# The query projection of a decode kernel, computed as rows in four column tiles and brought back to columns

## The chip, the cores and the metric

One core of one Trainium2 chip. The metric is device time in microseconds of one execution, as the median of several executions. The profiles are of single executions; their span is about 1.2 us shorter than the device time.

In the views, PE is the matrix engine and PEld its loading of weights; DVE, ACT and POOL are the vector, scalar and GpSimd engines; SPq is the queue of the engine that issues the loads. PSUM is the memory that PE writes its sums to, in banks. Times in a view, and all times of single packets and clock records told here, are us from the start of the span.

## The reference

One token attends over a cache of 65,536 keys, and an MLP mixer runs beside it. Only the first line below is touched by the change.

```python
q = ((x @ wq).reshape(B, Sq, Hq, Dh)).transpose(0, 2, 1, 3)   # x: 1x1x1024, wq: 1024x4096, 32 heads of 128
k = jnp.repeat(k_cache, rep, axis=1); v = jnp.repeat(v_cache, rep, axis=1)   # 4 KV heads, 65536 keys, rep = 8
scores = jnp.einsum("bhqd,bhkd->bhqk", q, k) * (Dh ** -0.5)
p = _softmax(scores, axis=-1)
o = jnp.einsum("bhqk,bhkd->bhqd", p, v)
# ... then o @ wo, and to it is added  x + B(layernorm(x)),  B a mixer MLP with w1, w2, w3, w4
```

Everything is bf16. K and V are 67 MB each, the weights together some 36 MB, and each byte is read once.

## The kernel before

The four first loads are issued at once, in one queue: both halves of wq into the second buffers of K and V, then the first K and V loads of 4 MB. A K or V load covers a pair of tiles; there are 32 tiles of 8,192 keys and 16 pairs.

```python
load_rows(Kn[:, 1, :], b_K[1], "wqa", A_wq, 0, 4)      # first half of wq, 4 MB
load_rows(Vn[:, 1, :], b_V[1], "wqb", A_wq, 4, 4)      # second half
issue_k(0)
issue_v(0)
# ... constants, layer norm of x ...
def mm_cols(ps_tile, c0, ncols, lhs_fn, rhs_fn, j0, nj, njt, bufs, b_ps):
    fns = []
    for j in range(j0, j0 + nj):
        for cx in range(ncols):
            fns.append(lambda e, j=j, cx=cx: e.matmul(ps_tile[:, c0 + cx:c0 + cx + 1], lhs_fn(j - j0, cx), rhs_fn(j),
                                                      start=(j == 0 and cx == 0), stop=(j == njt - 1), skip_group_check=True))
    _grp(q_pe, fns, reads=bufs, writes=[b_ps], partial=(j0 > 0))

for j0, t in ((0, Kn), (4, Vn)):       # 2 x 128 products: a 128x128 block of wq stationary, one column of x moving
    mm_cols(M1_ps, 0, HQ, ..., j0, 4, KT_D, (b_K[1] if j0 == 0 else b_V[1]) + [b_xn], b_M1)
issue_k(1)                             # second K load: its buffer held wq's first half
issue_v(1)
_op(q_dve, lambda e: e.tensor_copy(qT_bf[:], M1_ps[:, 0:HQ]), reads=[b_M1], writes=[b_qT])   # "q's cast"
# ... Yall from q (16 DVE products), layer norm for the MLP ...
for n in range(NT):                    # per tile: transposes of K on DVE (Ttr), scores on PE (QK), softmax, PV on PE
    QK(n); Ttr(n + 1, [0]); stats1(n); ...; PV(n); FLASH(n)
    # ... MLP and output weights are loaded and used in between ...
    if n % 2 == 0:
        issue_k(n // 2 + 2)            # a K buffer is free when the pair's transposes are done
    else:
        issue_v(n // 2 + 2)            # a V buffer when the pair's PV products are done
```

## Time and profile before

| | before |
|---|---|
| device time, median (3 runs) | 402.97 us (402.88 to 403.31) |
| DMA: bytes, share of 16 engines | 169.87 MB, 98.4% |
| busy: DVE, PE, POOL, ACT | 57%, 47%, 15%, 12% |
| q's cast | 27.91 us |
| third K load issued | 49.71 us |
| last weights used | 398.80 us |

The page of the kernel before, parts 2 and 3 (40 slices of 10 us, in tenths; then what DMA moved in each):

```profile
DMA  8999999999999999999999999999999999999995
q1 hardware_dynamic: 6920, 169.87, 98.4%
HBM read 169.87 MB, written 0.00 MB: 423 GB/s over the span
```

The table of windows (start:end, length, busy time and instructions of PE, PEld, DVE, ACT and POOL, then granted clock, DMA share, GB/s):

```profile
0.00:50.00 50.00, 14.74 (x308) 10.89 (x313) 18.95 (x54) 2.66 (x4) 6.42 (x29) 1.00 0.98 415
50.00:100.00 50.00, 20.73 (x215) 6.96 (x209) 30.34 (x53) 6.67 (x19) 8.17 (x9) 1.00 1.01 433
...
300.00:350.00 50.00, 21.42 (x194) 7.72 (x196) 33.94 (x55) 6.85 (x19) 6.88 (x8) 0.60 0.99 429
350.00:402.00 52.00, 28.98 (x320) 11.97 (x322) 23.86 (x43) 6.27 (x17) 8.67 (x9) 0.57 0.90 385
```

DMA never pauses: only the first and the last slice are below 9 tenths, and the rate is flat at some 430 GB/s. DVE, the busiest engine, has two fifths of the span to spare. (The granted clock of 1.00 in the first windows is not a measurement: the trace has no clock record before 105 us in this execution. The score products at 40.30 us below take the same 1.90 us as most do later under a recorded clock of 0.50.)

The timeline of the front (start, length, engine, line, operation, output<-inputs, count, idle time before it and what ended it):

```profile
18.73 3.55 PE L366 MATMUL M_ps<-xn_bf,Kn 128*128 128x1 bf16 x128 [0.57 <-DVE maskT L356]
22.38 0.33 SPq L286 DMA_DIRECT2D Kn<-in_A_k_cache_dram  x1
22.74 2.45 PE L366 MATMUL M_ps<-xn_bf,Vn 128*128 128x1 bf16 x86 [0.46 <-DMA Vn<-in_A_wq_dram]
26.59 1.28 PE L366 MATMUL M_ps<-xn_bf,Vn 128*128 128x1 bf16 x42 [1.39 <-issue]
27.91 0.19 DVE L375 CAST qT_bf<-M_ps 128x32 bf16<-128x32 f32 x1 [8.90 <-PE M_ps L366]
35.54 5.74 DVE L463 STREAM_TRANSPOSE X<-Kn 128x1024 f32<-128x1024 f32 x5
40.30 1.90 PE L475 MATMUL S_ps<-X,Yall 128*32 128x512 bf16 x16 [5.97 <-DVE X L463]
43.88 1.28 ACT L505 ACT_TABLE_LOAD   x1 [43.88 <-DVE brun L501]
49.71 0.33 SPq L286 DMA_DIRECT2D Kn<-in_A_k_cache_dram  x1
52.86 1.25 DVE L463 STREAM_TRANSPOSE X<-Kn 128x1024 f32<-128x1024 f32 x1 [3.23 <-DMA Kn<-in_A_k_cache_dram]
```

The projection waits for wq's second half, has a hole of 1.4 us, and its result goes through Yall and a layer norm to the first tile. But DVE, having done its first two tiles, then waits 3.23 us for the second K load.

The chain of waits (start, length, what), and the largest of DVE's waits (engine and tile, waited for: total us, times, longest):

```profile
22.74 2.45 PE M_ps L366 x86
25.20 1.39 issue
...
49.71 27.42 DMA Kn<-in_A_k_cache_dram
77.15 1.25 DVE X L463
```

```profile
DVE X L463 <- DMA Kn<-in_A_k_cache_dram: 64.5, 11, 10.0
```

The chain does pass through the projection. It says so because it follows each wait to its releaser: the transposes at 77.15 waited for a load that was issued at 49.71, and the issue waited for the first tiles. It does not say that the 27.42 us between are mostly time in a queue (its 4 MB need some 10 us at the rate of the windows).

### The profile page before, as it was taken

Reading aid. Unit: us, or ns where it says so; the run is one execution under the profiler, and the core shown is the slowest. Engines: PE = TensorE matmul, PEld = TensorE weight load, DVE = VectorE, ACT = ScalarE, POOL = GpSimd, SP = SyncE. Lnnn points to the kernel's source line nnn. Section 1 sums busy time; section 2 is a strip of 40 time slices with the busy share of each in tenths; the row PEclk is TensorE's granted clock in tenths of the full one; section 3 lists DMA queues with packets and bytes.
Section 4 is the critical chain, followed back from the end, with each engine's and each line's share of the span. In section 5 each row is a group of like instructions: output and inputs, shape, how many; then the busy total and the mean of one; then the engine's idle time right before and its main releaser. Section 6 shows DMA issues by size and latency. Waiting matters only on the chain.

```text
span 401.6 us, 5142 instructions
## 1 busy us (share of the span) xinstructions
PE 187.7 (47%) x2043; PEld 84.2 (21%) x2059; DVE 227.8 (57%) x400; ACT 48.4 (12%) x127; POOL 62.0 (15%) x90
## 2 busy tenths in 40 slices
PE   0361445064525745275630966353433545344674
PEld 0250111021103511062110731121111311111142
DVE  0217666277806588255753387676836775778410
ACT  0000211011101011011110011111201111112100
POOL 5000013011211011110310102111110102122110
PEclk9999999999855565555565555665565855656556
DMA  8999999999999999999999999999999999999995
GB/s 353 431 416 433 447 421 419 447 436 421 441 441 420 419 441 437 424 434 436 428 426 444 436 421 428 442 434 427 424 450 418 439 441 424 421 428 431 437 420 217
DMA packets 7088, 170.20 MB, mean 424 GB/s; under 512 B 916, under 2 KB 920, under 8 KB 1048
## 3 DMA queue, kind: packets, MB, share of 16 engines
q1 hardware_dynamic: 6920, 169.87, 98.4%
q8 instruction: 16, 0.26, 0.2%
q14 instruction: 8, 0.07, 0.0%
q10 hardware_dynamic: 144, 0.00, 0.0%
HBM read 169.87 MB, written 0.00 MB: 423 GB/s over the span
## 4 chain that ended last, share of the span: by engine, by line
DMA 54%; DVE 24%; PE 17%; issue 2%; ACT 2%; another core or an unknown queue 1%; SPq 0%; POOL 0%; ACTq 0%
DMA Kn<-in_A_k_cache_dram 43%; DVE X L463 12%; DMA Kn<-in_B_w_dram 6%; DMA Vn<-in_A_wq_dram 5%; PE H_ps L366 4%; DVE pT_f L516 3%; PE S_ps L475 3%; PE OT_ps L523 3%; DVE mrow L482 3%; PE M_ps L366 2%; ACT p_sb L505 2%; PE PT_ps L514 1%; PE M_ps L551 1%; PE OUT_ps L391 1%; DVE Yall L380 1%
## 5 line engine op out<-in xcount | busy, mean ns | idle before, releaser
L463 DVE STREAM_TRANSPOSE X<-Kn 128x1024 f32<-128x1024 f32 x128 | 151.7, 1215 | 64.5 <-DMA Kn<-in_A_k_cache_dram 64.5
L523 PE MATMUL OT_ps<-Vn,pT_f 128*32 128x512 bf16 x512 | 59.9, 620 | 54.1 <-DVE pT_f L516 54.1
L475 PE MATMUL S_ps<-X,Yall 128*32 128x512 bf16 x512 | 58.0, 598 | 17.0 <-DVE X L463 17.0
L488 PE MATMUL MB_ps<-Rm,Lmat 128*128 128x16 bf16 x32 | 6.2, 193 | 87.7 <-DVE Rm L483 87.7
L537 POOL TENSOR_TENSOR O_acc<-O_acc,tmpO 128x513 f32<-128x513 f32 x28 | 32.9, 1176 | 89.1 <-ACT tmpO L531 89.1
L535 POOL TENSOR_SCALAR O_acc<-O_acc,ff 128x513 f32<-128x513 f32 x28 | 19.6, 700 | 150.7 <-ACT ff L510 150.7
L505 ACT ACTIVATE p_sb<-S_ps,brun 128x512 bf16<-128x512 f32 x32 | 22.0, 688 | 173.1 <-DVE brun L503 154.6
L482 DVE TENSOR_REDUCE mrow<-S_ps 128x1 f32<-128x512 f32 x32 | 21.6, 674 | 24.6 <-PE S_ps L475 24.6
L531 ACT ACTIVATE tmpO<-OT_ps 128x512 f32<-128x512 f32 x32 | 19.2, 598 | 107.8 <-PE OT_ps L523 107.8
L475 PEld LDWEIGHTS S_ps<-X,Yall 128*32 128x32 bf16 x512 | 16.5, 126 | 54.7 <-DVE X L463 38.6
L516 DVE STREAM_TRANSPOSE pT_f<-PT_ps 128x512 f32<-128x512 f32 x32 | 22.9, 716 | 7.8 <-PE PT_ps L514 4.2
L523 PEld LDWEIGHTS OT_ps<-Vn,pT_f 128*32 128x32 bf16 x512 | 14.6, 128 | 59.4 <-DVE pT_f L516 42.7
L488 PEld LDWEIGHTS MB_ps<-Rm,Lmat 128*128 128x128 bf16 x32 | 3.3, 103 | 112.2 <-DVE Rm L483 112.2
L514 PE MATMUL PT_ps<-p_sb,permR 128*128 128x512 bf16 x16 | 9.5, 594 | 21.2 <-ACT p_sb L505 21.2
L366 PEld LDWEIGHTS H_ps<-xn_bf,W 128*128 128x128 bf16 x224 | 14.4, 172 | 1.7 <-issue 1.7
L366 PE MATMUL H_ps<-xn_bf,W 128*128 128x1 bf16 x224 | 14.5, 202 | 0.0
L514 PEld LDWEIGHTS PT_ps<-p_sb,permR 128*128 128x128 bf16 x32 | 3.4, 106 | 42.4 <-ACT p_sb L505 42.4
L492 DVE TENSOR_REDUCE Bst<-MB_ps 128x1 f32<-128x16 f32 x32 | 5.6, 174 | 8.3 <-PE MB_ps L488 8.3
L330 PE MATMUL M_ps<-ln_s,ones_f 128*128 128x1 f32 x6 | 1.8, 362 | 17.5 <-DVE ln_s L329 17.5
L533 POOL COPY O_acc<-tmpO 128x513 f32<-128x513 f32 x4 | 2.5, 615 | 47.5 <-ACT tmpO L531 47.5
L551 PE MATMUL M_ps<-O_acc,cb_W 128*128 128x128 f32 x32 | 7.4, 403 | 2.0 <-DVE cb_W L544 2.0
L391 PE MATMUL OUT_ps<-Kn,gh_bf 128*1 128x256 bf16 x112 | 5.8, 370 | 3.5 <-DMA Kn<-in_B_w_dram 3.5
(101 smaller groups left out, 114.0 us busy)
## 6 DMA issues: line engine op xcount, KB each, us to landing
Kn<-in_A_k_cache_dram SPq DMA_DIRECT2D x15, 4096.0 KB, 27.4
Vn<-in_A_v_cache_dram SPq DMA_DIRECT2D x15, 4096.0 KB, 22.3
W<-in_B_w_dram SPq DMA_DIRECT2D x2, 3584.0 KB, 25.1
W<-in_A_wo_dram SPq DMA_DIRECT2D x3, 2048.0 KB, 23.2
Kn<-in_A_wq_dram SPq DMA_DIRECT2D x1, 4096.0 KB, 12.3
Vn<-in_A_wq_dram SPq DMA_DIRECT2D x1, 4096.0 KB, 21.4
W<-in_B_w_dram SPq DMA_DIRECT2D x2, 2048.0 KB, 32.2
Kn<-in_A_k_cache_dram SPq DMA_DIRECT2D x2, 2048.0 KB, 24.8
```

The lines of the kernel that those rows point to most:

```text
L366: fns.append(lambda e, j=j, cx=cx: e.matmul(ps_tile[:, c0 + cx:c0 + cx + 1], lhs_fn(j - j0, cx), rhs_fn(j), start=(j == 0 and cx == 0), st ...
L463: _op(q_dve, lambda e, ix=ix: e.transpose(out=X32[:, xs, 1024 * ix:1024 * (ix + 1)], in_=Kn32[:, s, 4096 * half + 1024 * ix:4096 * half + ...
L475: fns.append(lambda e, we=we, cm=cm, mv=mv: e.matmul(S_ps[32 * cm:32 * cm + 32, :], Yall[:, h, we, :, :].rearrange("p a g -> p (a g)"), mv ...
L482: _op(q_dve, lambda e: e.reduce_max(mrow[:, m:m + 1], S_ps[:, :], axis=AX.X), reads=[b_S], writes=[b_mrow[m]])
L505: _op(q_act, lambda e: e.activation(p_sb[:, m, :], S_ps[:, :], ACTF.Exp, bias=brun[:, kn:kn + 1], scale=SCALE, accum_out=tmpO[:, m, 512:513]),
L514: _op(q_pe, lambda e: e.matmul(PT_ps[:, :], permR[:, :], p_sb[:, m, :], start=True, stop=True), reads=[b_p[m], b_const], writes=[b_PT])
L516: _op(q_dve, lambda e: e.transpose(out=pT_f[:, :], in_=PT_ps[:, :]), reads=[b_PT], writes=[b_pT])
L523: fns.append(lambda e, q=q, q4=q4: e.matmul(OT_ps[32 * q4:32 * q4 + 32, :], pT_bf[:, q, :, 1], Vn[:, s, 8192 * half + 512 * q:8192 * half ...
L531: _op(q_act, lambda e: e.activation(tmpO[:, m, 0:512], OT_ps[:, :], ACTF.Copy), reads=[b_OT], writes=[b_tmpO[m]], partial=True)
L535: _op(q_pool, lambda e: e.tensor_scalar(out=O_acc[:, :], in0=O_acc[:, :], scalar1=ff[:, m:m + 1], scalar2=0.0, op0=ALU.mult, op1=ALU.add), ...
L537: _op(q_pool, lambda e: e.tensor_tensor(out=O_acc[:, :], in0=O_acc[:, :], in1=tmpO[:, m, :], op=ALU.add), reads=[b_tmpO[m]], writes=[b_Oacc])
L551: fns.append(lambda e, t=t: e.matmul(M0_ps[:, 128:256], cb_W[:, t, :, :].rearrange("p g i -> p (g i)"), O_acc[:, t * P:(t + 1) * P], start ...
```

## The change

The intent is to spend less of PE's front on the projection. 256 products of one moving column, each with a fresh 128x128 block of wq as weights, become 64 products in which wq moves, 512 columns at a time, and x is the stationary side, broadcast to 32 columns. Four column tiles work at once, on four bands of 512 outputs, into two PSUM banks. q then lies in rows, so DVE and ACT each copy one bank, and eight products against columns of the identity matrix select one row of each band and bring q back to columns. The loads and their order stay as they were.

```diff
-        for j0, t in ((0, Kn), (4, Vn)):
-            mm_cols(M1_ps, 0, HQ, lambda j, cx, t=t: t[:, 1, j * HQD + cx * P:j * HQD + (cx + 1) * P], lambda j: xn_bf[:, j:j + 1], j0, 4, KT_D,
-                    (b_K[1] if j0 == 0 else b_V[1]) + [b_xn], b_M1)
+        q_banks = ((PT_ps, b_PT), (OT_ps, b_OT))
+        for j0, t, bt in ((0, Kn, b_K[1]), (4, Vn, b_V[1])):
+            fns = []
+            for j in range(j0, j0 + 4):
+                for b in range(2):
+                    for jj in range(4):
+                        fns.append(lambda e, j=j, b=b, jj=jj, j0=j0, t=t: e.matmul(
+                            q_banks[b][0][32 * jj:32 * jj + 32, :], xn_bf[:, j:j + 1].broadcast_to([P, 32]),
+                            t[:, 1, (j - j0) * HQD + 512 * (4 * b + jj):(j - j0) * HQD + 512 * (4 * b + jj + 1)],
+                            start=(j == 0), stop=(j == KT_D - 1), tile_position=(0, 32 * jj)))
+            _grp(q_pe, fns, reads=bt + [b_xn], writes=[b_PT, b_OT], partial=(j0 > 0))
         issue_k(1)
         issue_v(1)
+        _op(q_dve, lambda e: e.tensor_copy(p_sb[:, 0, :], PT_ps[:, :]), reads=[b_PT], writes=[b_p[0]])
+        _op(q_act, lambda e: e.activation(p_sb[:, 1, :], OT_ps[:, :], ACTF.Copy), reads=[b_OT], writes=[b_p[1]])
+        _grp(q_pe, [lambda e, b=b, i=i: e.matmul(M1_ps[:, 16 * b + i:16 * b + 16:4], p_sb[:, b, P * i:P * i + P], ident_bf[:, 0:97:32],
+                                                 start=(b + i == 0), stop=True, skip_group_check=True)
+                    for b in range(2) for i in range(4)], reads=b_p + [b_const], writes=[b_M1])
         _op(q_dve, lambda e: e.tensor_copy(qT_bf[:], M1_ps[:, 0:HQ]), reads=[b_M1], writes=[b_qT])
```

## The prediction

> **What bounds the kernel now.** DMA, nearly from end to end. The page gives 169.87 MB read at 423 GB/s over the 401.6 us span, the main queue's packets filling 98.4% of 16 engines. The table of windows shows 429 to 433 GB/s and a DMA share of 0.99 to 1.01 in every 50 us stretch from 50 to 350 us. The Trainium skill ("DMA: Bandwidth & Descriptors", "Where 436 GB/s comes from") puts the fabric's ceiling at 435.2 GB/s; this trace agrees, at 433. The time is about 2 us before the first big packet, 395 us of transfers without a gap, and 4 us from the last weights to the output. DVE is busy 57%, PE 47%; DVE waits 64.5 us for K tiles (the waits).
>
> **The touched stage** (timeline). PE multiplies the first half of wq from 18.70 to 22.28 us (128 one-column products), waits for the second half (22.74), multiplies it in 2.45 + 1.28 us around a hole of 1.48 us (released by "issue"); DVE casts q at 27.91. Then Yall (3.57 us), a layer norm, the first K transposes (35.5), the first score products (40.3).
>
> **Costs.**
> - Removed: 256 one-column products with 128-column weight loads, 7.28 us of PE, and probably the 1.48 us hole.
> - Added: 64 products of 512 columns, four column tiles at once: 16 rounds. The score products have this form: 16 products, 4 rounds, in 1.90 us, starts 0.43 us apart, as the skill ("TensorE: Matmul & The Clock Gate", Part 2, "Back-to-back issue gap": N/1.2 ns cold) states for 512 columns. Estimate: 3.6 us for the first half; 3.6 for the second, or 1.9 if the clock rises (some score groups take 0.97 to 1.3 us in the chain).
> - Added after it: two PSUM copies in parallel on DVE and ACT, 0.6 to 0.7 us (a 512-column ACT copy takes 0.60, a 512-column DVE reduction from PSUM 0.67), and eight selecting products, about 0.4.
> - Moved: ACT's first instruction becomes a copy at about 26 us, so the 1.28 us table load before the first exponential (43.9) may go there, off that chain.
>
> Sum: q's cast at 26 to 28 us instead of 27.91, first scores at 38.5 to 40.5, release of the first K buffer (third K load, issued at 49.71) 0 to 3 us earlier.
>
> **On the critical path: nothing, I expect.** The chain passes through these products, but then through 27.42 us of DMA after the K load issued at 49.71. Its 4 MB need about 10 us at 432 GB/s; the other 17 are queueing. The shortest such landing in the chain is 19.48 us, still 9 us of queue. The loads issued at 22.38 and 27.95 stand behind 16 MB that fill the queue until about 42 us. An earlier issue only waits longer. Bytes and tail (last weights at 398.8) are untouched.
>
> **Predicted:** 402.9 us, 80% range 402.1 to 403.7. Faster by over 2%: 0.01; within 2%: 0.98; slower: 0.01.
>
> **What would show it.** Right: 429 to 433 GB/s in the same windows; DVE's wait for K tiles grows by what the front saves; the second K tile (52.9) and the last weights (398.8) land within 0.5 us of before. A step is wrong if a projection half takes over 4.5 us, the hole stays, a second table load appears, or q's cast comes after 28.5.
>
> **What would make it wrong.** A late release that empties the queue (a DMA share under 0.9 over several us past 50), a front later by over 9 us, or wider PE reads lowering the DMA rate.

## The result, and the profile after

The changed kernel takes 402.95 us (402.77 to 403.10, 6 runs); the kernel before took 402.95 us (402.86 to 403.31, 6 runs). The ratio is 0.9999, with a 95% interval from 0.9986 to 1.0012: the same. Ratios here and below are the mean time of one kernel's runs over that of the other's of the same rounds, so not quite the ratio of the medians quoted.

The page after, the same lines:

```profile
DMA  8999999999999999999999999999999999999994
q1 hardware_dynamic: 6920, 169.87, 98.4%
HBM read 169.87 MB, written 0.00 MB: 423 GB/s over the span
```

The windows after:

```profile
0.00:50.00 50.00, 14.69 (x136) 6.29 (x137) 19.65 (x55) 3.25 (x5) 7.02 (x30) 0.78 0.98 417
50.00:100.00 50.00, 18.91 (x199) 6.54 (x201) 30.43 (x53) 6.77 (x20) 7.54 (x8) 0.57 1.00 432
...
300.00:350.00 50.00, 22.93 (x198) 8.19 (x204) 34.19 (x55) 7.11 (x19) 6.87 (x8) 0.57 1.00 430
350.00:402.00 52.00, 27.01 (x320) 10.79 (x318) 23.61 (x42) 6.00 (x17) 8.63 (x9) 0.60 0.90 383
```

The timeline of the front after; L376 is the new projection, each row four products that run at once:

```profile
17.88 0.62 PE L376 MATMUL PT_ps<-Kn,xn_bf 128*32 128x512 bf16 x4
18.28 0.64 PE L376 MATMUL OT_ps<-Kn,xn_bf 128*32 128x512 bf16 x4
...
22.54 0.40 PE L376 MATMUL PT_ps<-Vn,xn_bf 128*32 128x512 bf16 x4 [1.24 <-DMA Vn<-in_A_wq_dram]
22.77 0.39 PE L376 MATMUL OT_ps<-Vn,xn_bf 128*32 128x512 bf16 x4
...
24.51 0.69 DVE L383 CAST p_sb<-PT_ps 128x512 bf16<-128x512 f32 x1 [5.70 <-PE OT_ps L376]
25.66 0.19 DVE L388 CAST qT_bf<-M_ps 128x32 bf16<-128x32 f32 x1 [0.46 <-PE M_ps L385]
33.28 5.74 DVE L476 STREAM_TRANSPOSE X<-Kn 128x1024 f32<-128x1024 f32 x5
46.17 0.33 SPq L286 DMA_DIRECT2D Kn<-in_A_k_cache_dram  x1
52.98 1.25 DVE L476 STREAM_TRANSPOSE X<-Kn 128x1024 f32<-128x1024 f32 x1 [6.90 <-DMA Kn<-in_A_k_cache_dram]
```

The chain of waits and DVE's waits after:

```profile
46.17 30.96 DMA Kn<-in_A_k_cache_dram
77.15 1.25 DVE X L476
```

```profile
DVE X L476 <- DMA Kn<-in_A_k_cache_dram: 67.4, 11, 9.2
```

The projection did get shorter. Its second half takes 1.92 us (22.54 to 24.46) and the hole is gone. q's cast comes 2.25 us earlier. The table load of ACT moves to 1.22 us, off the first tile's chain, which gains another 1.28 us. So the third K load is issued 3.54 us earlier. And there it ends: the second K load lands when it did (52.98 against 52.86), DVE waits 6.90 us for it instead of 3.23, and the third one, issued 3.54 us earlier, is waited for 3.54 us longer (30.96 against 27.42), to the same 77.15 us. The products with the last weights start at 398.85 us, against 398.80.

### The profile page after: what moved, and what is told of

Same layout as the page of the kernel before. It is cut to its first block, busy times and chain, and to the rows that moved or that the text cites. A ratio compares the mean times of both kernels' runs of the same rounds, so it can differ in the third digit from the quotient of the medians.

```text
span 401.7 us, 4776 instructions
## 1 busy us (share of the span) xinstructions
PE 186.4 (46%) x1859; PEld 78.5 (20%) x1875; DVE 228.4 (57%) x401; ACT 48.9 (12%) x128; POOL 61.8 (15%) x90
## 4 chain that ended last, share of the span: by engine, by line
DMA 55%; DVE 24%; PE 16%; issue 2%; ACT 1%; SPq 0%; another core or an unknown queue 0%; POOL 0%; ACTq 0%
DMA Kn<-in_A_k_cache_dram 44%; DVE X L476 13%; DMA Kn<-in_B_w_dram 6%; DMA Vn<-in_A_wq_dram 5%; PE H_ps L366 4%; PE S_ps L488 3%; DVE pT_f L529 3%; PE OT_ps L536 3%; DVE mrow L495 3%; PE M_ps L366 1%; ACT p_sb L518 1%; PE PT_ps L527 1%; PE M_ps L564 1%; PE OUT_ps L404 1%; DVE Yall L393 1%
## 5 line engine op out<-in xcount | busy, mean ns | idle before, releaser
L488 PE MATMUL S_ps<-X,Yall 128*32 128x512 bf16 x512 | 59.1, 608 | 16.1 <-DVE X L476 16.1
L366 PEld LDWEIGHTS H_ps<-xn_bf,W 128*128 128x128 bf16 x224 | 14.4, 169 | 1.7 <-issue 1.7
```

Of the source, the lines that this page charges most:

```text
L488: fns.append(lambda e, we=we, cm=cm, mv=mv: e.matmul(S_ps[32 * cm:32 * cm + 32, :], Yall[:, h, we, :, :].rearrange("p a g -> p (a g)"), mv ...
```

## The experiments

The theory: the DMA queue is full from 2 us to the end and sets the time; whatever the front saves is spent waiting in front of that queue, and a front that is later is hidden in the same way until the queue runs dry. The main rival: the front is on the critical path, as the chain of waits suggests, and the change lost somewhere else what it saved there (wide PE reads that slow the DMA, or a throttled clock). For several of these runs the result differs from the reference; the comparison with the reference passed them all the same, so it says nothing about the attention's part at its tolerance.

### A later front: two, four, eight, sixteen and nine extra repeats

The changed kernel with the products of wq's first half run N extra times ahead of the real ones. The results stay correct, since each repeat begins its sums anew.

```diff
-        for j0, t, bt in ((0, Kn, b_K[1]), (4, Vn, b_V[1])):
+        for j0, t, bt in ((0, Kn, b_K[1]),) * N + ((0, Kn, b_K[1]), (4, Vn, b_V[1])):
+            n_q += 1
...
-                            start=(j == 0), stop=(j == KT_D - 1), tile_position=(0, 32 * jj)))
+                            start=(j == 0), stop=(j == KT_D - 1 or (fill and j == 3)), tile_position=(0, 32 * jj)))   # fill: n_q <= N
```

N = 2:

> The changed kernel with the products of the first half of wq run two extra times, results still correct. Each repeat should take 1.9 to 3.5 us of PE; about 1.2 us is absorbed while PE waits for the second half anyway, so q's cast comes about 3 to 6 us later than the 25.66 us of the changed kernel. Queue theory (the front of the kernel is hidden behind loads that are already queued): time within 0.5 us of 402.9; the third K load is issued at 49 to 52 us and still lands at 77.1. Rival (the front is on the critical path, and the change saved 2 to 3.5 us there but lost as much elsewhere): the time rises with the delay, to 406 to 409 us.

N = 4:

> As the run with two extra repeats, with four: q's cast about 9 to 13 us later. Queue theory: the second K load is issued at about 32 to 34 us, before the queue runs dry at about 42 us, and the third before 60 us, when the queue still holds work until 67: 402.9 us within 0.7. Rival: 412 to 416 us.

N = 8:

> With eight extra repeats: q's cast about 20 to 27 us later, the second K load issued at about 42 to 48 us, when the four first loads (16 MB) have just been done or are about to be: here the queue theory expects the first loss[...]: 403 to 411 us, equal to the length of the hole that the windows then show in the DMA between 40 and 50 us. Rival of a front on the critical path: 423 to 430 us. Rival that wide PE reads of SBUF slow the DMA: the windows from 20 to 40 us, filled with such products, fall under 420 GB/s instead of 425 to 435.

N = 16:

> With sixteen extra repeats at 1.98 us each (as the run with eight shows) the second K load is issued at about 54 us, while the first four loads are done at about 42. Queue theory: the queue runs dry from about 42 to 56 us, and the time rises by the length of that hole, to 414 to 419 us. If the front were hidden by something else than the queue, no such knee: 405 us or less; if the delay passed one to one from the start, 434 us or more.

The run with N = 9 was made after the one with N = 8, for the reason that its expectation tells:

> Why the run with eight extra repeats lost 1.0 us: its DMA shows no hole at 40 to 50 us, and its main queue moved each 8 MB as early as before to within 0.2 us up to 168 MB, but a 16 KB instruction fetch started at 397.98 us, and the last 4 KB packets of the last weights ended 1.15 us later than before. Fetch theory: one more repeat shifts PE's instruction pages by 64 instructions, so that the last fetch comes at about 395 to 397 us and the last weights land at 398.8 again: 402.6 to 403.2 us, faster than with eight repeats though the front is 2 us later. Queue theory for this loss (the later issues begin to starve the queue): 404.0 us or more, slower than with eight.

What was measured; the delay is q's cast against the 25.66 us of the changed kernel:

| extra repeats | delay at q's cast | second K load issued | device time, median (range) | ratio to before (95%) |
|---|---|---|---|---|
| 0 (changed kernel) | 0 | 21.42 | 402.95 (402.77 to 403.10) | 0.9999 (0.9986 to 1.0012) |
| 2 | 3.59 us | 26.09 | 403.00 (402.80 to 403.06) | 1.0001 (0.9989 to 1.0014) |
| 4 | 7.70 us | 30.20 | 402.92 (402.63 to 403.08) | 1.0001 (0.9988 to 1.0015) |
| 8 | 15.90 us | 38.40 | 403.92 (403.86 to 404.04) | 1.0025 (1.0013 to 1.0038) |
| 9 | 17.96 us | 40.46 | 404.86 (404.33 to 405.18) | 1.0047 (1.0035 to 1.0060) |
| 16 | 31.70 us | 54.20 | 418.16 (417.80 to 418.40) | 1.0377 (1.0361 to 1.0393) |

A front that is 7.70 us later costs nothing that can be measured. One that is 31.70 us later costs 15.2 us. So the delay is not passed on from the start, and the main rival falls: it asked for 412 us or more at four repeats. (The delays at four and eight came out below what was expected, 7.70 instead of 9 to 13 and 15.90 instead of 20 to 27, because the clock stayed up and a repeat took 1.98 us.) Where the cost of sixteen comes from is plain in the windows of that run; the last column is GB/s:

```profile
40.00:42.00 2.00, 1.93 (x36) 0.76 (x32) 0.00 (x0) 0.00 (x0) 0.00 (x0) 1.00 0.61 254
42.00:44.00 2.00, 1.93 (x36) 0.76 (x32) 0.00 (x0) 0.00 (x0) 0.00 (x0) 1.00 0.04 16
...
52.00:54.00 2.00, 1.93 (x36) 0.76 (x32) 0.00 (x0) 0.00 (x0) 0.00 (x0) 1.00 0.00 0
54.00:56.00 2.00, 1.83 (x36) 0.87 (x32) 0.00 (x0) 0.00 (x0) 0.00 (x0) 1.00 0.94 262
```

The four first loads are done at about 42 us, and the next one is issued at 54.20. Between them the DMA stands still. Summed over the packets of the trace, the main queue is 14.4 us behind the kernel before once 24 MB have moved, and stays 14.4 to 15.0 us behind to the end: in this kernel, what an empty queue lost was never won back. With nine repeats the second K load is issued at 40.46, just too late for a seamless change of loads, and the same sum is 0.8 us behind at 24 MB and 1.0 to 1.4 us behind from 32 MB on. With eight it is within 0.2 us of before at every 8 MB.

How the delay dies out shows in the start of the first transpose of each tile, against the kernel before (us, read from the traces; tiles 0 and 1 use the first K load, 2 and 3 the second, and so on):

```
tile                  0       1       2       4       6       8
changed kernel     -2.26   -2.26   +0.13   -0.01   -0.09   -0.09
8 extra repeats   +13.63  +13.63   +9.04   +0.47   +0.03   +0.11
9 extra repeats   +15.69  +15.69  +11.11   +3.10   +1.36   +1.14
```

The gain of 2.26 us is gone at the third tile, since that tile's K has not landed any sooner. The delay of 13.63 us needs until the fifth.

The repeats also test whether wide PE reads slow the DMA. These are the windows from 20 to 40 us of the kernel before, and then of the run with eight repeats:

```profile
20.00:40.00 20.00, 7.47 (x222) 6.95 (x219) 9.04 (x30) 0.00 (x0) 0.55 (x1) 1.00 0.98 420
```

```profile
20.00:40.00 20.00, 19.25 (x304) 7.50 (x296) 0.00 (x0) 0.00 (x0) 0.00 (x0) 1.00 0.98 419
```

PE streams wq for 19.25 of the 20 us, and the DMA moves 419 GB/s against 420. (The bar of 420 that the expectation set was too high for this stretch, in which before has 418 from 20 to 30 us too; the comparison is what counts.) The rival of a slowed DMA falls.

**The 1.0 us at eight repeats.** The queue explains no loss there, since its sum of bytes keeps to within 0.2 us. The tail does. This is the last group of products, of the kernel before and then of the run with eight repeats:

```profile
398.80 0.60 PE L391 MATMUL OUT_ps<-Kn,gh_bf 128*1 128x256 bf16 x8 [0.20 <-DMA Kn<-in_B_w_dram]
```

```profile
400.01 0.39 PE L406 MATMUL OUT_ps<-Kn,gh_bf 128*1 128x256 bf16 x8 [1.03 <-DMA Kn<-in_B_w_dram]
```

The products with the last 0.5 MB of weights start 1.2 us later, after a longer wait for them. In the packets of the trace, all but three of them end by 398.78, but the last three of 4 KB straggle to 399.54 (398.38 before), and a 16 KB instruction fetch for PE ran from 397.66 to 398.61, just ahead of these three. (The expectation's 397.98 us for this fetch was read on an axis 0.3 us later than that of the views.) The fetch theory said that nine repeats, by moving the fetch, would give 402.6 to 403.2 us. It gave 404.86, so that prediction fell. Its trace shows why it could not answer cleanly: the fetch had moved, to 395.29, and the straggling was gone (the last 4 KB packet ends 0.66 us after 169.8 MB have moved; 0.53 before, 1.60 with eight), but the same repeat had emptied the queue for the first time. One other trace, that of the changed kernel without V loads (told below), has a fetch as close before the end of its last weights, and it alone straggles alike: its last six 4 KB packets end 0.98 us apart, with eight repeats 1.08, in the other twelve traces 0.20 to 0.78. So the mechanism agrees with what the tails show, and as a cause of the 1.0 us it is not shown, since no run moves the fetch and changes nothing else.

### Less work for DVE

```diff
-            for ix in idx:
+            for ix in (idx if n < 2 else [i for i in idx if i == 0]):      # in Ttr(n, idx), kernel before
```

> The kernel before with three of the four DVE transposes of every K tile left out from the third tile on (wrong result on purpose; 90 of 128 transposes, about 109 us of DVE busy time, are gone; all loads remain). Queue theory: the DMA sets the time, so 402.9 us within 1.0, DVE's wait for K tiles grows by about 100 us. Rival (the chain through DVE and PE sets a good part of the time): at least 10 us faster.

It takes 402.76 us (402.57 to 402.88), ratio 0.9995 (0.9983 to 1.0008). DVE's busy time falls from 227.8 to 125.8 us, and the time does not move. DVE's costliest group on the page of this run (busy us, mean ns, then idle time before it and its releaser):

```profile
L463 DVE STREAM_TRANSPOSE X<-Kn 128x1024 f32<-128x1024 f32 x38 | 46.0, 1220 | 95.2 <-DMA Kn<-in_A_k_cache_dram 95.2
```

Of the 102 us saved, 30.7 went to waits for K tiles (95.2 against 64.5). I had expected about 100; the rest is spread over DVE's waits for PE within each tile, which are longer (for the scores 52.0 us instead of 24.6). This is the strongest form of the point: taking away nearly half of the busiest engine's work moves the median by 0.14 us, inside the scatter.

### A kernel in which the queue is not full

If the queue hides the front, then with fewer bytes the gain should appear. The first form loads V only for the first two pairs.

```diff
         def issue_v(m):
+            if m >= 2:
+                return
```

The form was run of the kernel before, of the changed kernel, and of the kernel before with one small ACT copy at its start, which takes only the table load out of the first tile's chain:

```diff
+        _op(q_act, lambda e: e.activation(cb_o[:, :], x_bf[:, :], ACTF.Copy), reads=[b_x], writes=[b_cb])
         load_rows(Kn[:, 1, :], b_K[1], "wqa", A_wq, 0, 4)
```

> The kernel before with V loaded only for the first two pairs of tiles and then reused (wrong result on purpose): 14 of 16 V loads and some 57 MB less, so that the DMA should no longer set the time and the chain through DVE and PE does. 310 to 345 us expected, with DVE's wait for K tiles under 15 us instead of 64.5. It is the base for the next two.

> The changed kernel with the same V loads left out. Queue theory: what the change saves at the front (2.25 us at q's cast, 3.5 us at the release of the first K buffer) is now on the critical path, so it is 2 to 4 us faster than the light form of the kernel before. Rival (the change has a hidden cost later, for example by the throttled clock, or the front saves nothing): within 1 us of it, or slower.

> The light form of the kernel before with one 8-column ACT copy at the very start, so that the table load of 1.28 us leaves the first tile's chain; the projection is as before. If the front's 3.5 us are 2.25 from the projection and 1.28 from the table load: about 1.3 us faster than the light form of the kernel before, so about a third of the gain of the light changed kernel.

They take 352.40 us (351.45 to 353.49), 353.16 us (351.90 to 353.90) and 351.42 us (351.02 to 352.71): within their own scatter, and no gain (and more than the 310 to 345 us expected of the first). But the form was badly chosen. DVE still waits for the second and third K load, up to 77 us:

```profile
77.15 1.25 DVE L478 STREAM_TRANSPOSE X<-Kn 128x1024 f32<-128x1024 f32 x1 [9.30 <-DMA Kn<-in_A_k_cache_dram]
```

That is the changed kernel's light form, and the light form of before has this line at 77.28. The two V loads that were left keep the early queue full, so these three runs decide nothing about it. Hence a second form, without any V load; the second product reads the wq rows in that buffer.

```diff
         def issue_v(m):
+            return
...
         def PV(n):
-            s, half = (n // 2) % 2, n % 2
+            s, half = 1, n % 2
```

> The light forms with V loaded twice could not answer the question: DVE still waited 12.4 to 14.4 us for the second and third K tile, up to 77 us, so the early queue still hid the front. Here the kernel before loads no V at all and the second product reads the wq rows that lie in that buffer (wrong result on purpose): the second K load lands at about 42 us and the third at about 62, before they are needed. Expected: 335 to 352 us, and DVE waits for K tiles under 3 us in all. Base for the next two.

> The changed kernel without V loads. Theory (the change saves 2.25 us at q's cast and 1.28 us at the table load, and only the full queue hides it): the first transpose of the fifth tile starts 3.0 to 4.0 us earlier than in the same form of the kernel before, and the time is 2 to 5 us shorter[...]. Rival (the saving is lost again after the front by some cost of the changed kernel itself): under 1 us shorter, with the fifth tile 3 us earlier.

> The kernel before without V loads and with one small ACT copy at the start, so that only the table load leaves the first tile's chain. If the front's gain is the sum of two parts: the fifth tile starts 1.1 to 1.5 us earlier than in that form of the kernel before, and the time is 0.5 to 2 us shorter.

Now DVE waits for no K tile at all in any of the three. The transposes that end with the fifth tile's first one, in the timelines of before, of the changed kernel and of the early table load in this form:

```profile
63.52 3.45 DVE L464 STREAM_TRANSPOSE X<-Kn 128x1024 f32<-128x1024 f32 x3
```

```profile
61.19 3.46 DVE L477 STREAM_TRANSPOSE X<-Kn 128x1024 f32<-128x1024 f32 x3
```

```profile
62.16 3.46 DVE L465 STREAM_TRANSPOSE X<-Kn 128x1024 f32<-128x1024 f32 x3
```

The changed kernel is 2.33 us ahead at the fifth tile, where the full kernel had nothing left at the third. The early table load alone is 1.36 us ahead, as expected. With the queue out of the way the front's gain outlives the third tile, and it is still 2.9 and 1.7 us at tile 16 (from the same starts in the traces). At the last tile it is 1.3 and 1.6 us: the changed kernel then leads by no more than the table load alone, so of the projection's own part nothing is left there in these profiles, and they do not show what it was lost to. In the times the gain is not resolved: 340.98 us (340.09 to 341.75), 340.18 us (338.23 to 340.55) and 341.70 us (339.55 to 342.03). I had expected 2 to 5 us for the changed kernel and 0.5 to 2 for the table load. The changed kernel's median is 0.80 us lower, which lies in the band of the rival that the expectation names (a saving lost again after the front), so this form does not exclude that rival. The scatter within a kernel, up to 2.5 us, is as large as the effect. Scores and PV products at two clock rates come to mind as its source, but no run tests that.

The lead at the fifth tile was expected to be 3 to 4 us. Why it is smaller can be read in the timeline of the changed kernel's form:

```profile
22.62 0.62 PE L377 MATMUL PT_ps<-Vn,xn_bf 128*32 128x512 bf16 x4 [1.06 <-DMA Vn<-in_A_wq_dram]
23.02 0.65 PE L377 MATMUL OT_ps<-Vn,xn_bf 128*32 128x512 bf16 x4
```

The rounds of the second half start 0.43 us apart here, and 0.22 us apart in the changed kernel above. The half takes 3.6 us instead of 1.9, and q's cast comes at 27.43 us, only 0.8 us before that of its base. In the changed kernel's profile the clock records begin with full speed at 21.0 us; here the first one is at 26.3 us.

## Why the prediction was right

**The time.** 402.95 us measured, 402.9 predicted, in a range from 402.1 to 403.7. The step that carries it, "on the critical path: nothing", was shown from three sides. A front up to 7.70 us later costs nothing, one that lets the queue run dry costs about the length of the hole (15.2 us of time, with the queue 14.4 to 15.0 us behind), and 102 us less DVE work changes nothing. The form without V loads adds that the gain outlives the third tile once the queue is no longer full, but not that it reaches the end. The Trainium skill ("DMA: Bandwidth & Descriptors", "Where 436 GB/s comes from") gives 435.2 GB/s as the ceiling, and the 429 to 433 GB/s from 50 to 350 us of the kernel before, and 430 to 433 of the changed one, agree with it.

**The removed part.** Right: 7.28 us of PE busy time and the hole went. The hole stood beside an instruction fetch. These are PE's 16 KB transfers up to 70 us in the two traces (start and length in us):

```
before   24.23 0.88    31.65 0.93    64.39 0.93
after    41.43 0.94
```

The hole lay from 25.20 to 26.59, just after the first. All six profiles with the old projection have such a hole, after the same 86 products of the second half, and it ends 2.3 to 2.4 us after the start of a fetch; none of the eight with the new projection has one there. The Trainium skill ("Runtime: NRT & Kernel Launch", "Instruction fetch mechanics") describes blocks of 16 KiB, 256 instructions, whose cost is "mostly hidden"; the transfers agree in size, and if the hole is the work of this one, it was not hidden. With fewer instructions the fetch comes later. That it is the cause of the hole was not tested by itself, and a fetch alone does not make one: with eight repeats the fetches at 28.3 and 36.4 us fell among the products, and the repeats went on at 1.98 us each.

**The added part.** Right in its structure, and its two branches both occurred: first half 3.4 us (3.6 predicted), second half 1.92 us in the changed kernel's profile (the branch "1.9 if the clock rises") and 3.6 us in the form without V loads. The Trainium skill ("TensorE: Matmul & The Clock Gate", Part 1) says that the window which raises the clock is free-running, so that the turn varies from run to run. These runs agree that it varies: it is first recorded at 21.0 us in one and 26.3 in the other, with the same PE instructions up to 21.0 us. The spread of 5 us is wider than the half microsecond that the page gives for its example. So the 1.92 us is what one profile caught; which branch the timed runs took is not known.

**The moved part.** The table load left the chain, as said, but it did not go to the copy at 24.5 us: it stands at 1.22 us, ahead of the wait of that copy. No second one appears.

**The sum at the front** was a little too modest: q's cast at 25.66 (26 to 28 predicted), first scores at 38.04 (38.5 to 40.5), third K load issued 3.54 us earlier (0 to 3). The terms were right, but adding them I rounded the good branch up and did not add the table load's 1.28 us to the 2.25 us of the projection.

**What would make it wrong** was mis-sized: "a front later by over 9 us". The front could be about 14 us later than before (15.90 later than after) with the queue still unbroken, though the time had by then risen by the 1.0 us of the tail. I had read the slack from the shortest landing of a K load, 19.48 us, that is from the queue in mid-kernel. The place that breaks first is the start, where the second K load has to be issued before the first 16 MB are through at about 42 us; in the kernel before it is issued at 22.38.

## What to carry to other kernels

A chain of waits that passes through a "DMA" piece far longer than its own bytes need is telling of a queue, and here nothing ahead of such a piece was worth speeding up: compare each landing with bytes over rate. Test it by a delay rather than by a gain, since a delay can be made as large as wanted. The slack is the delay at which the queue falls behind in the trace (here between 15.90 and 17.96 us); the time alone can mislead, as the 1.0 us at eight repeats did. When a full queue is lifted to see what it hid, check in the trace that the queue is really empty at the place in question, and expect other scatter to come forth.

## What the Trainium skill lacked or had wrong

- "Runtime: NRT & Kernel Launch", "Instruction fetch mechanics": the cost of crossing a block is called mostly hidden. Here a fetch of 16 KB took 0.88 to 0.97 us in the two kernels, whose DMA queue is full, and PE stood still for 1.4 us next to one of them (25.20 to 26.59 us); as its cause the fetch is not shown. The section has no word on fetches that share the DMA with a kernel's own loads. That the loads slow a fetch is not shown either: one in the empty queue of the run with sixteen repeats took 1.38 us.
- "TensorE: Matmul & The Clock Gate", "Weight-path perf modes": weights with a column step are said to be allowed in the fast load, and the section gives no price for it; no page gives a figure for weights read with a step ("SBUF — State Buffer" names a penalty for scattered reads, but no size). In the kernel before, 64 one-column products with contiguous weights took 1.81 us (28 ns each), and 64 with weights 8 elements apart took 3.96 us (62 ns each). In the trace of the changed kernel the two start 27 and 61 ns apart, both under a recorded clock of 0.50. This was read from the traces and not tested by itself.
- No page that this study drew on says how much a later start of compute may cost when loads are queued ahead. Here 7.70 us cost nothing, 15.90 us cost 1.0 us (in the tail, with the queue unbroken), 17.96 us cost 1.9 us and 31.70 us cost 15.2 us, with 16 MB queued at the start.
